# Reordering the opening of a fused attention and FFN kernel, and gating its last q tokens on the first weights

## The chip, the cores and the metric

One core of one Trainium2 chip. The metric is the device time of one execution in microseconds (us), lower is better. The fast executions of the kernel before lie between 326.11 and 326.97 us over all rounds; most kernels spread about as little, those with added dummy products up to 2 us. One run of the kernel before, of 372.13 us, with a low granted clock (0.851), is left out of every comparison.

## The reference

```python
pos = np.arange(S); theta = np.pi / 2.0 * pos / S
def phi(x): r = np.maximum(x, 0.0); return np.concatenate([r * cos_w, r * sin_w], axis=-1)
kv  = einsum('bhsf,bhsd->bhfd', phi(k), v);  z = sum of phi(k) over s
x   = (phi(q) @ kv) / (phi(q) @ z + 1e-6)      # [8 batches, 576 tokens, 8 heads x 64]
xn  = x / sqrt(mean(x*x) + 1e-6) * rms_g
g   = xn @ w_gate; out = (g * sigmoid(g) * (xn @ w_val)) @ w_out     # 512 -> 1536 -> 512
```

Everything is float32 outside and bf16 inside the products.

## The kernel before

The kernel loads k, q and v of batch 0, makes phi of them ("q_phi", "k_phi"), multiplies, divides, normalises token tiles of 128, transposes them on TensorE and feeds them to the FFN. Until the first token tile is normalised TensorE has little to do: this is the opening, about 30 us, with dummy products ("filler") that are meant to keep the clock up. After it TensorE is busy almost without a break. The parts that matter here:

```python
load_q_tokens(4, NJ)                 # tokens 4..8 of q, 640 KB, in the early queue
load_kv("k", 1, 0, 1)                # a quarter of k of batch 1
...
kvz_mm(0, low_banks, LOW)            # first half of phi(k)^T v
kvz_copy(A, 0, 0, low_banks[0], LOW); kvz_copy(A, 0, 1, low_banks[1], LOW)
v_cast(V, 0, 3, 4, 0, 5); v_cast(V, 0, 3, 4, 5, NJ)
...
filler(7, psV[1][:, :])
q_tr_pe(0, 2, psO[0][:, :])          # transposes of q tile 2
x_scale(0, 0)                        # normalise tile 0 (x * g was made ahead, x_gain)
...                                  # transposes of x tile 0, copies (x_tr)
q_phi(A, 0, 3, 1)                    # q tile 3, reads tokens 6 and 7
q_tr_evac(A, 0, 2, psO[0][:, :])
x_norm(0, 1)
q_phi(V, 0, 3, 0)
open_ffn(0, (0, 1), 0, 128)          # the first FFN products
x_tr_pe(0, 1, ...); x_tr_evac(V, 0, 1, ...)
q_tr_pe(0, 3, psO[1][:, :])
nd_pe(0, 2, psA); nd_post(0, 2, psA) # numerators of tile 2, division
q_tr_evac(A, 0, 3, psO[1][:, :])
open_ffn(0, (0, 1), 128, 256)
```

A is ScalarE, V is VectorE. In these traces the two work in the order in which their instructions are written: in the changed kernel ScalarE stands still for 5.0 us in front of one q_phi, with a copy that TensorE needs behind it.

Of the kernel before, what the change touches and what calls it, by code (L numbers as in the profile page):

```python
# [9 lines left out]
FP32 = mybir.dt.float32  # L10
# [16 lines left out]
def kernel(  # L27
# [11 lines left out]
    nc = tc.nc  # L39
# [34 lines left out]
    def load_kv(which, b, r0=0, r1=4, j0=0, j1=NJ):  # L74

        key = (which, b)
        if key not in raw:
            raw[key] = (two if which == "k" else one).tile(
                [P, 4, NJ * D], FP32, name=f"r{which}", tag=f"r{which}"
            )  # L80
        src = {"k": k, "v": v}[which]
        return nc.sync.dma_start(
            out=raw[key][:, r0:r1, j0 * D : j1 * D],
            in_=src[b, 2 * r0 : 2 * r1, :, :]
            .rearrange("h s d -> (h s d)")
            .rearrange("(r p n) -> p r n", p=P, n=NJ * D)[:, :, j0 * D : j1 * D],
        )
# [61 lines left out]
    def load_q_tokens(j0, j1):  # L149

        key = ("q", 0)
        if key not in raw:
            raw[key] = one.tile([P, 4, NJ * D], FP32, name="rq", tag="rq")
        return nc.sync.dma_start(
            out=raw[key][:, :, j0 * D : j1 * D],
            in_=q[0, :, :, :].rearrange("h s d -> (h s d)").rearrange(
                "(r p n) -> p r n", p=P, n=NJ * D
            )[:, :, j0 * D : j1 * D],
        )
# [7 lines left out]
    load_kv("v", 0, 2, 3)  # L167
    load_kv("v", 0, 3, 4, 0, 5)
    load_kv("v", 0, 3, 4, 5, NJ)
    load_q_tokens(4, NJ)  # L170
    load_kv("k", 1, 0, 1)
    nc.scalar.preload_act_table(AF.Silu)
    gb = one.tile([P, DM], FP32, name="gb")

# [106 lines left out]
            src = flat[:, 2048:2304].rearrange("p (i d) -> p i d", d=D)  # L281
        phi(eng, kp_of(b)[:, 8 * c : min(8 * c + 8, 36), o], src, f(c))

    def q_phi(eng, b, c, part):
        o = slice(0, D) if part == 0 else slice(D, F)
        f = cos_of if part == 0 else sin_of
        if (b, c) not in qp_tiles:
            qp_tiles[(b, c)] = four.tile(
                [P, H if c < 4 else 4, F], BF16, name="qp", tag="qp" if c < 4 else "qpt"
            )  # L290
        if b == 0:
            for i in range(2 if c < 4 else 1):
                j = 2 * c + i
                f = cos_of if part == 0 else sin_of
                phi(
                    eng, qp_tiles[(b, c)][:, 4 * i : 4 * i + 4, o],
                    raw[("q", 0)][:, :, j * D : (j + 1) * D], f(5 + j),
                )
            return
        src = view4(raw[("q", b)], c) if c < 4 else raw[("qt", b)][:, :, :]  # L300
        phi(eng, qp_tiles[(b, c)][:, :, o], src, f(c))
# [15 lines left out]
    def q_tr_pe(b, c, bank):  # L317
        t = qp_tiles[(b, c)]
        dst = bank.bitcast(BF16).rearrange("p (h s) -> p h s", s=P)
        for h in range(H if c < 4 else 4):  # L320
            nc.tensor.transpose(dst[:, h, :], t[:, h, :], ident[:, :])  # L321

    def q_tr_evac(eng, b, c, bank, heads=(0, 8)):
        h0, h1 = heads if c < 4 else (0, 4)
        if b == 0:
            src = bank.bitcast(BF16).rearrange("p (i h s) -> p h i s", i=2, h=H)
            copy(
                eng, q_dst(b, c)[:, h0:h1, :].rearrange("p h (i s) -> p h i s", i=2),
                src[:, h0:h1, :, :],
            )  # L330
            return
        dst = bank.bitcast(BF16).rearrange("p (h s) -> p h s", s=P)
        copy(eng, q_dst(b, c)[:, h0:h1, :], dst[:, h0:h1, :])
# [7 lines left out]
    def v_cast(eng, b, r0=0, r1=4, j0=0, j1=NJ):  # L341
        copy(
            eng, vvm[b % 2][:, r0:r1, j0:j1, 0:D],
            raw[("v", b)][:, r0:r1, j0 * D : j1 * D].rearrange("p r (j d) -> p r j d", d=D),
        )
# [50 lines left out]
    def kvz_copy(eng, b, c, bank, rs=(0, 4)):  # L396
        if (b, c) not in kvzs:
            kvzs[(b, c)] = three.tile([P, 4 * E], BF16, name="kvzs", tag=f"kvzs{c}")
        lo, hi = rs[0] * E, rs[1] * E
        copy(eng, kvzs[(b, c)][:, lo:hi], bank[:, lo:hi])  # L400
# [7 lines left out]
    def nd_pe(b, j, pst):  # L408

        o = headview(pst)  # L410
        for h in range(H):
            g, i = h // 4, h % 4
            if j < 4:
                nc.tensor.matmul(  # L414
                    o[:, g, i, :], lhsT=qpT[(b, 0)][:, h, j * P : (j + 1) * P],
                    rhs=kvz_of(b, h), start=True, stop=True,
                )
            else:
                for bb in (b - 1, b):
                    lo = 64 * (bb % 2)  # L420
                    r, c = (h // 2, h % 2) if bb == 0 else (i, g)
                    nc.tensor.matmul(  # L422
                        o[lo : lo + 64, g, i, :],
                        lhsT=qpT[(bb, 1)][:, r, 64 * c : 64 * c + 64],
                        rhs=kvz_of(bb, h), start=True, stop=True,
                    )
# [59 lines left out]
        rs_of[(b, j)] = rs  # L486

    xn_of = {}
    xg = three.tile([P, DM], FP32, name="sg", tag="sg")

    def x_gain(b, j, g):

        c = slice(g * DM // 2, (g + 1) * DM // 2)
        nc.vector.tensor_tensor(
            out=xg[:, c], in0=x_of[(b, j)][:, c], in1=gb[:, c], op=ALU.mult
        )

    def x_scale(b, j):
        xn = four.tile([P, DM], BF16, name="xn", tag="xn")
        nc.vector.tensor_scalar(  # L500
            out=xn[:, :], in0=xg[:, :], scalar1=rs_of[(b, j)][:, :], scalar2=None, op0=ALU.mult
        )
        xn_of[(b, j)] = xn

    def x_norm(b, j):
        xn = four.tile([P, DM], BF16, name="xn", tag="xn")
        nc.vector.scalar_tensor_tensor(  # L507
# [26 lines left out]
    def x_tr_evac(eng, b, j, bank, part=(0, 4)):  # L534
        dst = bank.bitcast(BF16).rearrange("p (t s) -> p t s", s=P)
        copy(eng, x_dst(b, j)[:, part[0] : part[1], :], dst[:, part[0] : part[1], :])
# [54 lines left out]
    def filler(n, bank):  # L591
        for _ in range(n):
            nc.tensor.matmul(bank, lhsT=warm[:, 0:P], rhs=warm[:, :], start=True, stop=True)  # L593
# [25 lines left out]
    def gval_slice(c0, c1):  # L619
        weight_dmas.append(weight_slice(wg, moe_w_gate, c0, c1))  # L620
        weight_dmas.append(weight_slice(wv, moe_w_val, c0, c1))
# [4 lines left out]
    )  # L626
    gval_slice(256, 512)
    gval_slice(512, 768)

    wo_dmas = []  # L630

# [19 lines left out]
    low_banks = [psG[1][:, :], psV[1][:, :]]  # L651
    high_banks = [psA[:, c, :] for c in range(2)]
    kvz_mm(0, low_banks, LOW)
    kvz_copy(A, 0, 0, low_banks[0], LOW)
    kvz_copy(A, 0, 1, low_banks[1], LOW)
    v_cast(V, 0, 3, 4, 0, 5)
    v_cast(V, 0, 3, 4, 5, NJ)
    kvz_mm(0, high_banks, (2, 3))
    nd_half(0, 0, 0, psV[0])
    nd_post_half(0, 0, 0, psV[0])  # L660
    x_gain(0, 0, 0)
    q_tr_evac(A, 0, 1, psO[0][:, :], (0, 4))
    kvz_mm(0, high_banks, (3, 4))
    kvz_copy(A, 0, 0, high_banks[0], HIGH)
    kvz_copy(A, 0, 1, high_banks[1], HIGH)
    filler(1, idle)
    nd_half(0, 0, 1, psO[1])
    nd_post_half(0, 0, 1, psO[1])
    q_tr_evac(A, 0, 1, psO[0][:, :], (4, 8))
    q_phi(A, 0, 2, 1)  # L670
    x_sq(0, 0)
    nd_pe(0, 1, psA)
    nd_post(0, 1, psA)
    x_gain(0, 0, 1)
    q_phi(A, 0, 2, 0)
    x_sq(0, 1)
    gval_slice(768, 1152)
    gval_slice(1152, 1536)
    filler(7, psV[1][:, :])
    q_tr_pe(0, 2, psO[0][:, :])  # L680
    x_scale(0, 0)

    def open_ffn(pair, steps, c0, c1, first=0, parts=(0, 1)):

        x = xnT[0]
        for i, n in enumerate(steps):
            for a in parts:
                w = (wg, wv)[a]
                bank = pairs[pair][a]
                lo = 256 * (first + i) + c0 % 256  # L690
                for t in range(NDT):
                    nc.tensor.matmul(  # L692
                        bank[:, lo : lo + c1 - c0],
                        lhsT=w[:, t, n * P : (n + 1) * P], rhs=x[:, t, c0:c1],
                        start=(t == 0), stop=(t == NDT - 1),
                    )
# [16 lines left out]
        x_tr_pe(0, 0, bank[:, :], part)  # L713
        x_tr_evac(eng, 0, 0, bank[:, :], part)
    q_phi(A, 0, 3, 1)
    q_tr_evac(A, 0, 2, psO[0][:, :])
    x_norm(0, 1)
    q_phi(V, 0, 3, 0)
    open_ffn(0, (0, 1), 0, 128)
    x_tr_pe(0, 1, psV[1][:, :])  # L720
    x_tr_evac(V, 0, 1, psV[1][:, :])
    q_tr_pe(0, 3, psO[1][:, :])
    nd_pe(0, 2, psA)
    nd_post(0, 2, psA)
    q_tr_evac(A, 0, 3, psO[1][:, :])
    x_sq(0, 2)
    wo_load(0)
    open_ffn(0, (0, 1), 128, 256)
    open_ffn(1, (2,), 0, 256, parts=(0,))
    nd_pe(0, 3, psA)  # L730
    nd_post(0, 3, psA)
    open_ffn(1, (3,), 0, 256, first=1, parts=(0,))
    x_norm(0, 2)
    open_ffn(1, (2, 3), 0, 256, parts=(1,))
    open_h(0, 0, 0)
# [34 lines left out]
    def at(blk, n, where, f, *args):  # L770
        slots.setdefault((blk, n), none())[where].append((f, args))
# [2 lines left out]
        for f, args in slots.get((blk, n), none())[where]:  # L774
            f(*args)

    d = load_kv("k", 1, 1, 4)
    tc.add_manual_dep(d.ins, weight_dmas[5].ins.name, SYNC_DEP, reason="after most weights")
    gate_q = load_q(1)
    tc.add_manual_dep(  # L780
# [10 lines left out]
    for j in range(NJ):  # L791
        at(0, 7 + max(0, j - 1) // 2, "post", k_phi, V, 1, j, 0)
        at(0, 7 + max(0, j - 1) // 2, "post", k_phi, A, 1, j, 1)
    at(0, 10, "post", q_phi, V, 1, 0, 0)
    at(0, 11, "post", q_phi, A, 1, 0, 1)


# [216 lines left out]
```

## Time and profile before

| | before |
|---|---|
| time, median | 326.53 us |
| span of the profiled run | 324.5 us |
| TensorE busy, granted clock | 97%, 0.999 |
| first FFN product | 17.26 us |
| start of the main loop | 29.98 us |
| from there to the end | 294.5 us |

TensorE bounds the kernel, so two numbers say most: when the main loop starts, and how long it is from there to the end. The lines that show it are in the prediction.

### The profile page before, as it was taken

The page shows a single profiled execution, that of the slowest core. Times are in us where ns is not written, and L with a number is a line of the kernel's source. Part 1 is how long each engine was busy: PE and PEld are TensorE (multiplying, and loading weights), DVE is VectorE, ACT ScalarE, POOL GpSimd, SP SyncE. Part 2 cuts the span into 40 slices and gives each one's busy share as a digit, 9 for nine tenths or more (in the row PEclk, how much of TensorE's full clock was granted, in tenths as well). Part 3 has the DMA queues.
Part 4 walks back from the last instruction along what each step waited for, and adds up shares of the span by engine and source line. Part 5 has one row for each costly group of instructions (what it writes and reads, how often), then busy time and mean ns, then how long its engine had stood idle before and what let it go on. Part 6 is the DMA issues. An engine that isn't in the chain of part 4 may idle for free.

```text
span 324.5 us, 6131 instructions
## 1 busy us (share of the span) xinstructions
PE 316.2 (97%) x2249; PEld 162.4 (50%) x2284; DVE 184.3 (57%) x398; ACT 173.8 (54%) x351; POOL 39.3 (12%) x85
## 2 busy tenths in 40 slices
PE   8999999999999999999999999999999999999995
PEld 3588465555445444554454445444544444444443
DVE  6875768787656765578267745772577133203410
ACT  6974865965665556645555466455644333223321
POOL 4660202001111110012001120120011000000000
PEclk9999999999999999999999999999999999999999
DMA  7999999898799775977597679856611400020014
GB/s 271 281 196 253 309 205 339 243 165 189 164 248 273 190 205 153 237 163 195 165 214 206 155 219 210 194 158 215 128 40 33 131 32 0 25 106 0 1 33 100
DMA packets 89377, 53.90 MB, mean 166 GB/s; under 512 B 56321, under 2 KB 81921, under 8 KB 89346
## 3 DMA queue, kind: packets, MB, share of 16 engines
q1 hardware_dynamic: 82304, 48.65, 57.4%
q0 software_dynamic: 6880, 4.72, 10.0%
q8 instruction: 18, 0.29, 0.4%
q10 hardware_dynamic: 162, 0.13, 0.2%
q14 instruction: 13, 0.11, 0.1%
HBM read 37.75 MB, written 9.44 MB: 145 GB/s over the span
## 4 chain that ended last, share of the span: by engine, by line
PE 93%; DVE 2%; ACT 2%; issue 1%; POOL 0%; DVEq 0%
PE psC L566 26%; PE psV L546 26%; PE psG L546 26%; PE psA L414 2%; PE psO L593 2%; PE psA L370 2%; PE psG L566 2%; PE psO L692 1%; PE psG L692 1%; PE psV L692 1%; PE psV L321 1%; ACT kpm L252 1%; PE psA L386 1%; ACT sg L555 0%; PE psA L422 0%
## 5 line engine op out<-in xcount | busy, mean ns | idle before, releaser
L561 DVE TENSOR_TENSOR hT<-psV,sg 128x512 bf16<-128x512 f32 x102 | 70.3, 689 | 96.0 <-PE psV L546 71.2
L555 ACT ACTIVATE sg<-psG 128x512 f32<-128x512 f32 x102 | 60.6, 594 | 64.5 <-PE psG L546 63.2
L546 PE MATMUL psV<-xnT,wv 128*128 128x512 bf16 (+1 forms) x365 | 92.1, 375 | 0.4
L546 PE MATMUL psG<-xnT,wg 128*128 128x512 bf16 (+1 forms) x352 | 90.9, 375 | 0.7
L566 PE MATMUL psC<-wo,hT 128*128 128x512 bf16 x382 | 88.2, 380 | 0.7
L546 PEld LDWEIGHTS <-wv 128*128 128x128 bf16 x416 | 40.6, 98 | 47.4
L566 PEld LDWEIGHTS <-hT 128*128 128x128 bf16 x420 | 40.2, 98 | 46.7
L546 PEld LDWEIGHTS <-wg 128*128 128x128 bf16 x416 | 38.5, 98 | 40.8 <-DVE xnT L339 0.4
L485 POOL TENSOR_TENSOR rs<-ms,mhalf 128x1 f32<-128x1 f32 x36 | 19.8, 549 | 187.6 <-ACT scr L480 187.6
L337 ACT COPY osb<-psC 128x512 f32<-128x512 f32 (+1 forms) x33 | 19.1, 579 | 43.1 <-PE psC L566 42.4
L507 DVE SCALAR_TENSOR_TENSOR xn<-xt,rs,gb 128x512 bf16<-128x512 f32 x35 | 26.5, 757 | 16.4 <-POOL rs L485 16.3
L480 ACT ACTIVATE scr<-xt 128x513 bf16<-128x513 f32 x36 | 22.9, 635 | 23.7 <-DVE xt L469 23.6
L252 ACT ACTIVATE kpm<-rk,tab 128x256 bf16<-128x256 f32 (+2 forms) x58 | 28.2, 545 | 1.5 <-DMA rk<-in_k_dram 1.5
L469 DVE TENSOR_TENSOR xt<-psA,rec 128x512 f32<-128x512 f32 x35 | 24.2, 691 | 1.2
L252 ACT ACTIVATE qp<-rq,tab 128x512 bf16<-128x512 f32 (+1 forms) x37 | 23.7, 661 | 0.0
L254 DVE TENSOR_SCALAR kpm<-rk,tab 128x128 bf16<-128x128 f32 (+2 forms) x64 | 20.5, 377 | 2.1 <-DMA rk<-in_k_dram 2.1
L254 DVE TENSOR_SCALAR qp<-rq,tab 128x512 bf16<-128x512 f32 (+1 forms) x37 | 16.0, 452 | 0.0
L414 PEld LDWEIGHTS <-qpT 128*128 128x128 bf16 x248 | 11.7, 98 | 6.7 <-issue 0.3
L414 PE MATMUL psA<-kvzs,qpT 128*128 128x65 bf16 x248 | 12.8, 194 | 0.3
L546 PE MATMUL psG<-xnt_tail,wg 128*128 128x512 bf16 x48 | 12.3, 379 | 0.1
L546 PE MATMUL psV<-xnt_tail,wv 128*128 128x512 bf16 x47 | 12.1, 379 | 0.0
L339 DVE CAST vvm<-rv 128x1024 bf16<-128x1024 f32 (+4 forms) x16 | 10.4, 674 | 0.0
(99 smaller groups left out, 183.8 us busy)
## 6 DMA issues: line engine op xcount, KB each, us to landing
out_dram<-osb SPq DMA_DIRECT2D x28, 256.0 KB, 2.5
rk<-in_k_dram SPq DMA_DIRECT2D x20, 256.0 KB, 3.2
rq<-in_q_dram SPq DMA_DIRECT2D x20, 256.0 KB, 3.1
rv<-in_v_dram SPq DMA_DIRECT2D x16, 256.0 KB, 3.2
rq<-in_q_dram SPq DMA_DIRECT2D x2, 1024.0 KB, 9.2
out_dram<-osb SPq DMA_DIRECT2D x14, 128.0 KB, 3.2
rv<-in_v_dram SPq DMA_DIRECT2D x3, 576.0 KB, 8.4
wo<-in_moe_w_out_dram POOLq DMA_DIRECT2D x4, 384.0 KB, 7.1
```

Of the source, the lines that this page charges most:

```text
L252: nc.scalar.activation(out=out_ap, in_=in_ap, func=AF.Relu, scale=scale)
L254: eng.tensor_scalar(out=out_ap, in0=in_ap, scalar1=scale, scalar2=0.0, op0=ALU.mult, op1=ALU.max)
L337: nc.scalar.copy(out=o, in_=i)
L414: nc.tensor.matmul(o[:, g, i, :], lhsT=qpT[(b, 0)][:, h, j * P : (j + 1) * P], rhs=kvz_of(b, h), start=True, stop=True,)
L469: nc.vector.tensor_tensor(out=xt[:, 0:DM].rearrange("p (b h d) -> p b h d", b=2, d=D), in0=o[:, :, :, 0:D], in1=rec[:, :, :].unsqueeze(3). ...
L480: nc.scalar.activation(out=scr[:, :], in_=xt[:, 0 : DM + 1], func=AF.Square, scale=1.0 / math.sqrt(DM), accum_out=ms[:, :],)
L485: nc.gpsimd.tensor_tensor(out=rs[:, :], in0=ms[:, :], in1=mhalf[:, :], op=ALU.pow)
L507: nc.vector.scalar_tensor_tensor(out=xn[:, :], in0=x_of[(b, j)][:, 0:DM], scalar=rs_of[(b, j)][:, :], in1=gb[:, :], op0=ALU.mult, op1=ALU. ...
L546: nc.tensor.matmul(pst[bank][:, cols[0] : cols[1]], lhsT=w[:, t, n * P : (n + 1) * P], rhs=x[:, t, cols[0] : cols[1]], start=(t == 0), sto ...
L555: nc.scalar.activation(out=sg[:, :], in_=psG[bank][:, :], func=AF.Silu)
L561: nc.vector.tensor_tensor(out=hTs[blk][:, n, :], in0=psV[bank][:, :], in1=sg[:, :], op=ALU.mult)
L566: nc.tensor.matmul(bank, lhsT=hTs[blk][:, n, j * P : (j + 1) * P], rhs=wo[:, n, :], start=(n == 0), stop=(n == NNT - 1),)
```

## The change

The intent, as the edit suggests it: get the early queue shorter so that weights come sooner (the last q tokens wait for the first weight slice: this wait is called the gate below), swap a v cast and two copies between ScalarE and VectorE, move half of q tile 2's phi from ScalarE to VectorE, and start the FFN products ahead of q tile 2's transposes. A step of the normalisation (x_gain, x_scale) is dropped for the plain x_norm, k of batch 1 comes in one piece, and one q_phi of batch 1 moves a step later.

```diff
-    load_q_tokens(4, NJ)
-    load_kv("k", 1, 0, 1)
+    load_q_tokens(4, 6)
...
     gval_slice(512, 768)
+    d = load_q_tokens(6, NJ)
+    tc.add_manual_dep(d.ins, weight_dmas[0].ins.name, SYNC_DEP, reason="after the first weights")
...
-    kvz_copy(A, 0, 0, low_banks[0], LOW)
-    kvz_copy(A, 0, 1, low_banks[1], LOW)
-    v_cast(V, 0, 3, 4, 0, 5)
+    kvz_copy(V, 0, 0, low_banks[0], LOW)
+    kvz_copy(V, 0, 1, low_banks[1], LOW)
+    v_cast(A, 0, 3, 4, 0, 5)
...
-    x_gain(0, 0, 1)
-    q_phi(A, 0, 2, 0)
+    q_phi(A, 0, 2, 1, (1,))
+    q_phi(V, 0, 2, 0, (0,))
+    x_norm(0, 0)
+    q_phi(V, 0, 2, 0, (1,))
...
-    filler(7, psV[1][:, :])
-    q_tr_pe(0, 2, psO[0][:, :])
-    x_scale(0, 0)
+    filler(9, psV[1][:, :])
...
     q_phi(A, 0, 3, 1)
-    q_tr_evac(A, 0, 2, psO[0][:, :])
     x_norm(0, 1)
-    q_phi(V, 0, 3, 0)
     open_ffn(0, (0, 1), 0, 128)
     x_tr_pe(0, 1, psV[1][:, :])
     x_tr_evac(V, 0, 1, psV[1][:, :])
+    q_tr_pe(0, 2, psO[0][:, :])
+    q_tr_evac(A, 0, 2, psO[0][:, :])
+    q_phi(V, 0, 3, 0)
+    open_ffn(0, (0, 1), 128, 256)
     q_tr_pe(0, 3, psO[1][:, :])
     nd_pe(0, 2, psA)
...
-    open_ffn(0, (0, 1), 128, 256)
...
-    d = load_kv("k", 1, 1, 4)
+    d = load_kv("k", 1)
...
-    at(0, 10, "post", q_phi, V, 1, 0, 0)
+    at(0, 11, "post", q_phi, V, 1, 0, 0)
```

Left out of the diff: the removal of x_gain and x_scale themselves, the first x_gain, one filler, the first `q_phi(A, 0, 2, 1)` cut to its first half, the new argument of q_phi that names the half, and an FFN step moved from behind nd_pe(0, 3) to before it.

More of the change, by code (lines that the diff above doesn't have):

```diff
@@ L282, in k_phi_as_q, with q_phi @@
         phi(eng, kp_of(b)[:, 8 * c : min(8 * c + 8, 36), o], src, f(c))
-    def q_phi(eng, b, c, part):
+    def q_phi(eng, b, c, part, subs=(0, 1)):
         o = slice(0, D) if part == 0 else slice(D, F)
@@ L291, in q_phi @@
         if b == 0:
-            for i in range(2 if c < 4 else 1):
+            for i in subs if c < 4 else (0,):
                 j = 2 * c + i
@@ L488 @@
     xn_of = {}
-    xg = three.tile([P, DM], FP32, name="sg", tag="sg")
-    def x_gain(b, j, g):
-        c = slice(g * DM // 2, (g + 1) * DM // 2)
-        nc.vector.tensor_tensor(
-            out=xg[:, c], in0=x_of[(b, j)][:, c], in1=gb[:, c], op=ALU.mult
-        )
-    def x_scale(b, j):
-        xn = four.tile([P, DM], BF16, name="xn", tag="xn")
-        nc.vector.tensor_scalar(
-            out=xn[:, :], in0=xg[:, :], scalar1=rs_of[(b, j)][:, :], scalar2=None, op0=ALU.mult
-        )
-        xn_of[(b, j)] = xn
     def x_norm(b, j):
@@ L628 @@
     gval_slice(512, 768)
+    d = load_q_tokens(6, NJ)
+    tc.add_manual_dep(
+        d.ins, weight_dmas[0].ins.name, SYNC_DEP, reason="after the first weights"
+    )
     wo_dmas = []
@@ L660 @@
     nd_post_half(0, 0, 0, psV[0])
-    x_gain(0, 0, 0)
     q_tr_evac(A, 0, 1, psO[0][:, :], (0, 4))
@@ L665 @@
     kvz_copy(A, 0, 1, high_banks[1], HIGH)
-    filler(1, idle)
     nd_half(0, 0, 1, psO[1])
@@ L669 @@
     q_tr_evac(A, 0, 1, psO[0][:, :], (4, 8))
-    q_phi(A, 0, 2, 1)
+    q_phi(A, 0, 2, 1, (0,))
     x_sq(0, 0)
@@ L727 @@
     wo_load(0)
-    open_ffn(0, (0, 1), 128, 256)
     open_ffn(1, (2,), 0, 256, parts=(0,))
+    open_ffn(1, (3,), 0, 256, first=1, parts=(0,))
     nd_pe(0, 3, psA)
     nd_post(0, 3, psA)
-    open_ffn(1, (3,), 0, 256, first=1, parts=(0,))
     x_norm(0, 2)
```

## The prediction

> **What bounds the kernel now.** I read the page first (busy shares, slices, chain), then the chain in order of time, then the timeline of the first 30 us, then what the DMA queues moved in short windows. From the page:
>
> ```profile
> span 324.5 us, 6131 instructions
> ...
> PE 316.2 (97%) x2249; PEld 162.4 (50%) x2284; DVE 184.3 (57%) x398; ACT 173.8 (54%) x351; POOL 39.3 (12%) x85
> ...
> PEclk9999999999999999999999999999999999999999
> ...
> PE 93%; DVE 2%; ACT 2%; issue 1%; POOL 0%; DVEq 0%
> ```
>
> TensorE is busy 97% of the span at a full granted clock and holds 93% of the chain that ended last. The change touches only the first 30 us and some loads; from there the stream of products is the same. So the time moves only by how much earlier or later TensorE gets through the opening, one to one. The opening's own chain shows where it waits for others:
>
> ```profile
> 14.56 0.72 ACT scr L480 x2
> ...
> 16.77 0.56 POOL rs L485
> 17.33 0.02 issue
> 17.36 0.75 DVE xn L507
> 18.11 0.82 DVE qp L254 x2
> 18.93 0.14 issue
> 19.07 0.38 PE psO L321 x4
> 19.45 0.25 PE psA L414 x8
> ```
>
> From 19.07 us on the opening's chain is TensorE alone; the stretch from 19.3 to 30.0 us has 10.70 us of TensorE busy in 10.70. Before that, TensorE is kept occupied by dummy products (fillers) and waits for token tile 0 to be normalised:
>
> ```profile
> 15.37 0.57 POOL L485 TENSOR_TENSOR rs<-ms,mhalf 128x1 f32<-128x1 f32 x1 [0.65 <-ACT scr L480]
> ...
> 15.97 0.49 DVE L500 TENSOR_SCALAR xn<-sg,rs 128x512 bf16<-128x512 f32 x1
> ...
> 16.51 0.28 PE L532 MATMUL psG<-ident,xn 128*128 128x128 bf16 x2
> ...
> 17.10 0.91 ACT L252 ACTIVATE qp<-rq,tab 128x256 bf16<-128x256 f32 x2
> 17.26 0.38 PE L692 MATMUL psG<-xnT,wg 128*128 128x128 bf16 x4 [0.35 <-ACT xnT L337]
> ```
>
> The first FFN product starts at 17.26 and waits for xnT on ScalarE, not for weights: the first gate slice, issued at 10.07, landed 4.9 us later, at 14.97; the first value slice (11.00 + 6.0) at 17.0. No TensorE wait on a DMA is in the waits of the first 40 us. The line at 17.10 is where tokens 6 and 7 of q are first read.
>
> **What the Trainium skill says.** (1) "DMA: Bandwidth & Descriptors", section "Queues, rings and completion order": each DMA engine takes turns between the queue rows that have work, a packet at a time. In the trace, the hardware queue (k of batch 1, 864 KB) and the software queue (weights) in 26.25 to 29.5 us:
>
> ```profile
> q1 hardware_dynamic: 325, 0.75, 66.0%
> q0 software_dynamic: 331, 0.25, 48.1%
> ```
>
> One packet each in turn, so that agrees. But that load was issued at 22.46 and the hardware queue moved nothing from 22.5 to 26 us, while weights ran: 3.5 us to its first packet. (2) The same page, "Anatomy of one DMA — SWDGE (gpsimd) path", puts about 2 us of fixed cost on one transfer. For the gated q load of batch 1 (issued at 30.84) the first packet came about 2 us later, so the trace gives 2 to 3.5 us, before any data. (3) "VectorE: DVE Perf Modes", "Why `tensor_tensor` can't do 2×_2P or 4×": two tensor inputs leave no read port for a double rate. The trace agrees: 757 ns for the 128x512 normalisation with two tensors, 486 ns for the scaling with one. (4) "TensorE: Matmul & The Clock Gate", "What's actually happening": the clock drops to half after about 3.4 us without work. The first 15 fillers took 6.01 us (0.4 each), later ones 0.21 each, which fits; no drop later is in the trace before.
>
> **The change part by part.**
>
> *LOW copies to VectorE, first piece of the last v cast to ScalarE.* A 128x260 copy from PSUM on VectorE took 427 ns and a 128x512 one 692, a slope of 1.05 ns per element, so 128x130 is estimated at 0.29 us, as against 0.27 on ScalarE. VectorE starts the next instruction some 0.08 us before the last ends, so: last LOW product 11.58, copies to 12.10, then the remaining cast (284 ns) to 12.30. Before, both casts were done at 11.99, and the HIGH products began at 12.26, behind the half of numerators that waits for the copies. Now they begin at about 12.34. Cost 0.08.
>
> *x_gain removed, x_scale becomes x_norm.* Two VectorE products of 0.42 go. The first sat in 13.30 to 13.72, just ahead of the reciprocal of the second half (13.64). With it gone the second half can start as soon as its numerators end: 13.50 + 0.08 = 13.58, so the 0.08 is won back, and x_sq stays at about 14.55, rs at 15.94. The second lay under the wait for rs and was free. Its replacement there, one q_phi of 0.35 on VectorE (15.42 to 15.77), is free too. But after rs the normalisation takes 0.757 in place of 0.486: 15.97 to 16.72. Cost 0.25: transposes at 16.76, first FFN product at 17.26 + 0.25 = 17.51.
>
> *q tile 2's transposes moved behind the first FFN products.* Eight transposes are 0.45 us of TensorE (chain: psO L321 x8, 0.45). They ran at 15.74, in time otherwise empty; the fillers grow from 8 to 9 to cover it. Now they lie in the busy stretch: 0.45 us more of work there. The useful work from the first FFN product to the first step of the main loop sums to 12.20 before (24 groups, 0.22 for four 128-column products, 0.44 for four of 256, 0.45 for eight transposes, 0.25 for eight numerators) out of 12.72 elapsed (17.26 to 29.98), so 0.52 was waiting. It becomes 12.65.
>
> *Numerators of tile 2 come later.* They stood after x_tr(1) and q tile 3 and ended at 19.70; now q tile 2 and FFN columns 128 to 256 (0.89) come first. With nothing waiting for q: FFN 17.51 to 18.40, x_tr(1) to 18.62, q tile 2 to 19.07, wait for xnT to 19.30, FFN to 20.19, q tile 3 to 20.64, numerators end at about 21.05. From there to the transposes of x tile 2 there is a chain of 3.53 us (before: 19.70 to 23.23): divide, square, power, nd_post of tile 3, normalise. TensorE has 2.91 us of work to cover it (0.88 + 0.29 + 0.87 + 0.87), as against 3.8 before. So x tile 2 is transposed at 24.58 and not 23.3: 1.25 us late, even with q in time.
>
> *The last q tokens gated on the first gate slice.* Out of the early queue go 384 KB of q and 288 KB of k. The weights hardly gain: their first packet came at 12.0, and the hardware queue was nearly empty by 12.4, so about 0.4 us: slice at 14.5. The q load is then issued at 14.5; first packet 2 to 3.5 us later, 16.5 to 18; 512 packets of 768 B over 16 engines, 32 each, alternating with weight packets. A weight packet took 16/370 us = 43 ns, a 768 B packet at the early rate of 390 GB/s 32 ns; 32 pairs are 2.4 us. End at 18.9 to 20.4, landing some 0.5 to 1 later: 19.4 to 21.4, middle 20.2. It is read at 17.10 (ScalarE) and 18.03 (VectorE) now. ScalarE is in order, so the copy of q tile 2 stands behind it: landing 20.2, two q_phi of 0.9 to 21.1, copy of 1.0 to 22.1, numerators of tile 2 to 22.5 in place of 21.05. That adds 1.45.
>
> *k of batch 1 in one piece, q_phi of batch 1 a step later.* 288 KB more behind the weights, landing about 33 in place of 31.0; it is first read at 33.26, and everything before that shifts later as well. Off the path.
>
> **Sum:** 1.25 + 1.45 = 2.7 us late by the working, of 326.6: 329.3. The gate could be less late than I put it, so I take 328.5.
>
> **Rivals.** *A: q lands in time.* The early queue is lighter, the first slice could land before 14, and a first packet after 2 us and a short drain give 18.9. For: the author moved q tile 3 behind more FFN work, as if they knew. Against: 3.5 us to a first packet in the trace. Then the loss is 1.25, or 0.5 if the chain to x tile 2 is shorter than before: 327.1 to 327.9. *B: the change gains.* The chain ahead of the first FFN product could shrink by more than the 0.25 that x_norm costs, as ScalarE is freed of the LOW copies and of half of q_phi. For: the chain of waits runs through just that q_phi at 15.28. Against: the sums of ScalarE at 14.56 wait for xt on VectorE, not for ScalarE; and the saved wait is at most the 0.52 us in the busy stretch. Time 326.0 to 326.5. *C: the clock.* A wait of 2 us with breaks around it could bring TensorE to half rate for some 3.4 us, a cost of 1.7 more: 330.5 to 331.
>
> **Range and chances.** Between B's end and C's start: 326.4 to 330.6. A 2% gain needs 6.5 us, more than half of the opening's busy stretch and 0.52 us of it is wait: 0.01. A 2% loss needs C and a late q together: 0.03. Within 2%: 0.96. I put 0.75 on slower at all.
>
> **What would show it.** In the changed profile: first FFN product near 17.5; normalisation of tile 0 at 0.75; the q load of 384 KB issued near 14.5 and landing near 20; a wait of ScalarE and VectorE on the DMA of rq ahead of q_phi; a hole in TensorE of 1 to 2 us between 20 and 23, and a second of 0.6 before the transposes of x tile 2; the main loop starting near 32.3 and not 29.98; the same length after it. I am wrong if no wait on rq is there, or if the first FFN product is earlier than 17.2, or if the distance from the main loop's start to the end differs by over 0.5 us.

## The result

| | before | changed |
|---|---|---|
| time, median of 6 | 326.53 us | 332.59 us |
| span of the profiled run | 324.5 us | 330.9 us |
| granted clock | 0.999 | 0.994 |
| first FFN product | 17.26 | 17.81 |
| start of the main loop | 29.98 | 35.74 |
| from there to the end | 294.5 | 295.2 |

The ratio is 1.0186, 95% interval 1.0173 to 1.0199. Ratios here are the mean time of one kernel's fast runs over that of the other's of the same rounds, so not quite the ratio of the medians. The change makes the kernel 6.06 us slower, and the measured time lies above the range of the prediction. Of the 6.4 us between the spans, 5.76 are there when the main loop starts; 0.64 come later. The weights hardly gained: the first slice landed at 14.65 and not 14.97, and no compute engine had waited for it.

The page of the changed kernel:

```profile
span 330.9 us, 6164 instructions
...
PEclk9998999999999999999999999999999999999999
...
PE 88%; DMA 6%; DVE 2%; ACT 2%; issue 1%; SPq 0%; DVEq 0%
```

A DMA share of 6% has come into the chain that ended last, and one slice of the clock is below 9 tenths. The opening's part of that chain, in order of time (start, length, what):

```profile
2.27 7.63 DMA rv<-in_v_dram
9.91 0.30 issue
10.21 4.45 DMA wg<-in_moe_w_gate_dram
14.65 0.02 issue
14.67 8.07 DMA rq<-in_q_dram
22.75 0.02 issue
22.77 0.91 ACT qp L251 x2
23.67 0.91 ACT qpT L336
24.58 0.05 issue
24.62 0.62 PE psA L413 x8
```

Three loads stand in a row: the first v, the weight slice gated on it, the q load gated on the slice. That last one took 8.07 us from issue to landing. Before, the first v and the slice were no part of the chain, which had TensorE's dummy products and the VectorE and ScalarE steps there. The waits of the first 48 us that bear on it (engine, who, for whom: total, times, longest), first of the kernel before:

```profile
PEld L321 <- ACT qp L252: 0.9, 2, 0.7
...
PE psO L321 <- DVE qp L254: 0.2, 1, 0.2
```

and of the changed kernel:

```profile
ACT qp L251 <- DMA rq<-in_q_dram: 5.0, 1, 5.0
...
DVE qp L253 <- DMA rq<-in_q_dram: 3.2, 1, 3.2
...
PE psO L320 <- ACT qp L251: 2.7, 1, 2.7
...
PE psV L320 <- DVE qp L253: 0.5, 1, 0.5
```

ScalarE and VectorE wait for q, TensorE waits behind ScalarE for 2.7 us. The last line is another wait, in the main loop at 47 us. TensorE in single microseconds of the changed kernel (stretch, length, busy, instructions, granted clock, DMA share, GB/s):

```profile
20.00:21.00 1.00, 0.66 (x12) 1.00 1.25 238
21.00:22.00 1.00, 0.00 (x0) 1.00 1.31 239
22.00:23.00 1.00, 0.00 (x0) 1.00 1.43 197
23.00:24.00 1.00, 0.67 (x7) 0.64 1.34 202
24.00:25.00 1.00, 0.74 (x11) 0.50 1.32 204
25.00:26.00 1.00, 1.00 (x10) 0.50 1.31 202
26.00:27.00 1.00, 1.00 (x14) 0.66 1.32 204
27.00:28.00 1.00, 1.00 (x15) 1.00 1.30 230
```

A hole of 2.7 us (20.66 to 23.33), and some 3.4 us at half clock (23.27 to 26.69, by finer windows). Before, these microseconds are full at clock 1.00; two of them:

```profile
22.00:23.00 1.00, 1.00 (x11) 1.00 1.32 204
24.00:25.00 1.00, 1.00 (x17) 1.00 1.35 215
```

What the two DMA queues moved between the issue of the q load and its landing (packets, MB, share), q1 being the hardware queue with q and q0 the weights; first 14.5 to 18.5 us, then 18.5 to 22.5:

```profile
q0 software_dynamic: 1196, 0.60, 127.3%
```

```profile
q0 software_dynamic: 1011, 0.50, 92.0%
q1 hardware_dynamic: 528, 0.39, 39.4%
```

q moved nothing in the first of these. By finer windows its first packet came at 18.73, 4.1 us after the issue at 14.67; until then some 1230 weight packets went through 16 DMA engines, 77 each. Then its 528 packets shared the engines with the weights for 3.8 us, and 0.2 later it had landed.

### The profile page after: what moved, and what is told of

Its sections match the earlier page's. It is cut to its first block, busy times and chain, and to the rows that moved or that the text cites. A ratio compares the mean times of both kernels' runs of the same rounds, so it can differ in the third digit from the quotient of the medians.

```text
span 330.9 us, 6164 instructions
## 1 busy us (share of the span) xinstructions
PE 320.3 (97%) x2285; PEld 163.5 (49%) x2285; DVE 184.9 (56%) x399; ACT 173.1 (52%) x348; POOL 39.3 (12%) x85
## 4 chain that ended last, share of the span: by engine, by line
PE 88%; DMA 6%; DVE 2%; ACT 2%; issue 1%; SPq 0%; DVEq 0%
PE psC L549 26%; PE psG L529 26%; PE psV L529 25%; DMA rq<-in_q_dram 2%; PE psA L413 2%; DMA rv<-in_v_dram 2%; PE psA L369 2%; DMA wg<-in_moe_w_gate_dram 1%; PE psG L549 1%; PE psG L677 1%; PE psO L677 1%; ACT kpm L251 1%; PE psV L320 1%; PE psA L385 1%; DVE hT L544 1%
## 5 line engine op out<-in xcount | busy, mean ns | idle before, releaser
L529 PE MATMUL psG<-xnT,wg 128*128 128x512 bf16 (+1 forms) x368 | 92.8, 374 | 0.1
L549 PE MATMUL psC<-wo,hT 128*128 128x512 bf16 x396 | 89.4, 379 | 0.0
L490 DVE SCALAR_TENSOR_TENSOR xn<-xt,rs,gb 128x512 bf16<-128x512 f32 x36 | 27.3, 757 | 16.5 <-POOL rs L484 16.5
L251 ACT ACTIVATE qp<-rq,tab 128x512 bf16<-128x512 f32 (+1 forms) x35 | 22.9, 670 | 5.0 <-DMA rq<-in_q_dram 5.0
L253 DVE TENSOR_SCALAR kpm<-rk,tab 128x128 bf16<-128x128 f32 (+2 forms) x64 | 20.5, 378 | 2.3 <-DMA rk<-in_k_dram 2.3
L253 DVE TENSOR_SCALAR qp<-rq,tab 128x512 bf16<-128x512 f32 (+1 forms) x39 | 16.4, 441 | 3.2 <-DMA rq<-in_q_dram 3.2
L338 DVE CAST vvm<-rv 128x1024 bf16<-128x1024 f32 (+3 forms) x15 | 10.3, 709 | 0.0
```

The lines of the kernel that those rows point to most:

```text
L251: nc.scalar.activation(out=out_ap, in_=in_ap, func=AF.Relu, scale=scale)
L253: eng.tensor_scalar(out=out_ap, in0=in_ap, scalar1=scale, scalar2=0.0, op0=ALU.mult, op1=ALU.max)
L490: nc.vector.scalar_tensor_tensor(out=xn[:, :], in0=x_of[(b, j)][:, 0:DM], scalar=rs_of[(b, j)][:, :], in1=gb[:, :], op0=ALU.mult, op1=ALU. ...
L529: nc.tensor.matmul(pst[bank][:, cols[0] : cols[1]], lhsT=w[:, t, n * P : (n + 1) * P], rhs=x[:, t, cols[0] : cols[1]], start=(t == 0), sto ...
L549: nc.tensor.matmul(bank, lhsT=hTs[blk][:, n, j * P : (j + 1) * P], rhs=wo[:, n, :], start=(n == 0), stop=(n == NNT - 1),)
```

## The experiments

Theory: the gate makes most of the loss, because a load on the hardware queue that is issued behind a backlog of weight packets waits for them; the reordering and the moved q_phi make the rest. Rivals: the reordering makes most of it; or the half clock does; or a load simply takes this long.

**1. Gate undone.** From the changed kernel:

```diff
     load_q_tokens(4, 6)
+    load_q_tokens(6, NJ)
...
-    d = load_q_tokens(6, NJ)
-    tc.add_manual_dep(d.ins, weight_dmas[0].ins.name, ...)
```

> The changed kernel with the gate alone undone: the q load of 384 KB stands in the early queue right after its sister of 256 KB. Theory (the gate makes the loss): no wait on the DMA of rq, no hole in TensorE after 20 us, clock 1.00 throughout; what is left is the reordering, the later first product (17.8) and the longer normalisation: 326.5 + 1.25 + 0.3 = 328.1 us, between 327.5 and 328.5. Rival (the reordering and the other parts hold most of the 6 us): 331 or more.

Measured: 328.26 us (ratio 1.0055, 1.0039 to 1.0071), main loop at 31.24, clock 1.00, no engine waits for rq ahead of q_phi. So the gate is worth 332.59 - 328.26 = 4.3 of the 6.1 us (4.3 by the ratios too). The main loop starts 1.26 later than before, where the prediction's working without a late q had 1.25. The remaining 0.6 us lie after that.

**2. Gate alone, on the kernel before.**

```diff
-    load_q_tokens(4, NJ)
+    load_q_tokens(4, 6)
...
+    d = load_q_tokens(6, NJ)
+    tc.add_manual_dep(d.ins, weight_dmas[0].ins.name, ...)
```

> The kernel before with the gate alone added (q tokens 4 and 5 early, 6 to 8 after the first gate slice). Theory: q lands near 22.7; in the order of before the transposes of q tile 3 come 1.3 us of TensorE work earlier, so the hole is longer (18.6 to 23.3), the numerators of tile 2 end near 25.0 in place of 19.7, and the clock falls: 326.5 + 5.3 + about 2 = 333.8 us, between 332.5 and 335. Rival (gate harmless without the reordering): 326.5 to 328.

Measured: 333.34 us (ratio 1.0208, 1.0192 to 1.0224), main loop at 37.22. The gate alone costs 6.8 us, more than the whole change: the order of before has less TensorE work to do until q arrives. The reordering of the change thus hides part of what its gate costs. TensorE here:

```profile
20.00:21.00 1.00, 0.00 (x0) 1.00 1.24 242
21.00:22.00 1.00, 0.00 (x0) 0.89 1.33 227
22.00:23.00 1.00, 0.00 (x0) 0.50 1.42 200
...
27.00:28.00 1.00, 1.00 (x10) 0.50 1.26 251
```

It is idle from 18.96, and the clock falls at 21.77, 2.8 us later; in the changed kernel it fell 2.6 us into the hole. The Trainium skill ("TensorE: Matmul & The Clock Gate", "What's actually happening") names an idle window of about 3.4; both falls came sooner than that.

**3. Gate moved to the first v load.**

```diff
-    tc.add_manual_dep(d.ins, weight_dmas[0].ins.name, ...)
+    tc.add_manual_dep(d.ins, first_v.ins.name, ...)
```

> The changed kernel with the q load gated on the first v load (landed 10.2) and not on the first gate slice (14.65). Theory A (a load on the hardware queue waits behind the weight packets already queued on each DMA engine): issued at 10.2, ahead of all weight packets, its first packet comes about 2 us later, it lands before 16, no engine waits for it and the time is that of the ungated kernel within 0.3 us. Theory B (8 us from issue to landing whatever else is queued): lands at 18.3, q_phi of tile 3 waits 0.5 us, time 0.3 to 0.8 us over the ungated one.

Measured: 328.52 us (ratio 1.0066, 1.0048 to 1.0084). The load was issued at 9.67 and landed 3.4 us later:

```profile
rq<-in_q_dram SPq DMA_DIRECT2D x1, 384.0 KB, 3.4
```

Issued ahead of every weight packet (their first came after 12.25), though with its own queue's earlier loads still running, the same 384 KB took 3.4 and not 8.07 us, which rules out that the load takes 8 us in any case. No engine waits for it.

**4. Gate kept, backlog taken away.**

```diff
     gval_slice(0, 256)                       # gated on v, as before
+    d = load_q_tokens(6, NJ)                 # gated on the first slice, as in the change
     gval_slice(256, 512)
+    tc.add_manual_dep(weight_dmas[2].ins, d.ins.name, ...)
     gval_slice(512, 768)
```

> The changed kernel, gate kept, but the weight slices after the first pair wait until the gated q load has landed, so that only one slice is queued when q is issued at about 14.6. The time is not the question (the later slices come late, 330 to 334 us). Theory A (q waits behind the weight packets that are already queued when it is issued): first q packet about 2 us after issue, landing at 18.5 or earlier, 4 us from issue. Theory B (4 us to the first packet in any case): first packet at 18.5, landing after 20, 6 us or more from issue.

Measured: issued at 13.80, landed 3.8 us later (time 335.77 us, one run of unknown state: GpSimd stood 6.65 us until q had landed, to issue the next slice, and only then made the `rs` that the first normalisation needs, so the first FFN product came at 23.15; the time says nothing here, the queues do). The queues from the issue to 14.75 us, and from there to 17.5:

```profile
q0 software_dynamic: 289, 0.14, 110.3%
```

```profile
q1 hardware_dynamic: 528, 0.39, 54.2%
q0 software_dynamic: 1, 0.00, 0.1%
```

The q packets begin 1.0 us after the issue, when the 289 packets left of the one queued slice (18 an engine) are through. So how long q waits depends on what is queued ahead of it. But it does not wait for all of it. What was queued can be estimated from the sizes (512 packets for a slice of 256 KB, 768 for one of 384 KB, from 0.60 MB in 1196 packets) less the packets already moved; the 36 are counted, and the 165 leave out a slice of w_out that was just being issued:

| load, kernel | weight packets an engine queued at the issue (estimate) | moved before its first packet | wait for its first packet |
|---|---|---|---|
| gated q, this experiment | 18 | 18 | 1.0 us |
| q of batch 1, kernel before (30.84) | 36 | 29 | 2.1 us |
| gated q, changed kernel | 144 | 77 | 4.1 us |
| k of batch 1, kernel before (22.46) | 165 | 60 | 3.6 us |

Where the limit lies and what sets it stays open.

**5. q_phi of batch 1 back at its step**, on the ungated kernel:

```diff
-    at(0, 11, "post", q_phi, V, 1, 0, 0)
+    at(0, 10, "post", q_phi, V, 1, 0, 0)
```

> The ungated kernel with VectorE's first q_phi of batch 1 put back at step 10 (the change had moved it to step 11). Theory: in the changed kernel the transposes of q tile 0 of batch 1 wait 0.48 us for that q_phi, and from the main loop's start to the end it is 295.16 us against 294.52 before; with the move undone the wait goes and the time falls by 0.6 us from the ungated 328.26, to 327.65. Rival (the 0.6 us comes from the later k and v loads): no change, 328.2.

Measured: 327.57 us (ratio 1.0037, 1.0024 to 1.0051), 0.7 below the ungated kernel, or 0.6 by the ratios, as the two ran in different rounds. From the main loop to the end it is 294.5 again, and the wait `PE psV L320 <- DVE qp L253`, which the ungated kernel still had, is gone; a move of one instruction by one step is worth a tenth of the whole loss.

**6. TensorE's order of before as well**, on the last kernel: q tile 2's transposes ahead of the first FFN products, numerators of tile 2 ahead of FFN columns 128 to 256. Left out of this diff: the same for one FFN step and nd_pe(0, 3), and VectorE's order, which went back with it (q_phi of tile 2 whole ahead of the first x_norm, q_phi of tile 3 right after the second).

```diff
-    filler(9, psV[1][:, :])
+    filler(7, psV[1][:, :])
+    q_tr_pe(0, 2, psO[0][:, :])
...
+    q_tr_evac(A, 0, 2, psO[0][:, :])         # after q_phi(A, 0, 3, 1), as before
...
-    q_tr_pe(0, 2, psO[0][:, :])
-    q_tr_evac(A, 0, 2, psO[0][:, :])
-    open_ffn(0, (0, 1), 128, 256)
     q_tr_pe(0, 3, psO[1][:, :])
     nd_pe(0, 2, psA)
...
+    open_ffn(0, (0, 1), 128, 256)
```

> As the last one, and TensorE's order of before as well: q tile 2's transposes ahead of the first FFN products, numerators of tile 2 ahead of FFN columns 128 to 256. Theory (the reordering costs its 0.45 us of transposes in the busy stretch and 0.6 us ahead of x tile 2): main loop starts at 30.2 and not 31.24, time 326.7 us, within 0.3 of the kernel before; what is left of the loss is the 0.2 us of the longer normalisation. Rival (the first part, casts and copies, holds a further loss): 327.3 or more.

Measured: 326.42 us (ratio 1.0005, 0.9992 to 1.0017). The reordering, TensorE's and VectorE's together, is worth 327.57 - 326.42 = 1.15 us. What is left of the change (casts, copies, the longer normalisation, k in one piece) cannot be told from nothing; the 0.2 us expected of the normalisation are within the noise.

**7. Dummy products in the hole**, 13 and then 9, in the changed kernel:

```diff
+    filler(13, psO[1][:, :])                 # or 9
     q_tr_pe(0, 3, psO[1][:, :])
```

> The changed kernel with 13 dummy products of 128x512 in the hole ahead of q tile 3's transposes (13 x 0.216 = 2.8 us, no longer than the hole itself). Theory: some 1.7 us of the 6.06 is the half clock from 23.4 to 26.7; the dummies keep the clock at 1.00, q lands as late as ever (22.7): 332.6 - 1.7 = 330.9 us. Rival (clock is no cost, or follows the transposes): 332.6 unchanged.

Measured: 332.69 us (331.32 to 333.32; ratio 1.0184, 1.0153 to 1.0215). The clock stayed at 1.00, the median did not fall. The profiled run is the fastest of the four, 331.32: its gate opened earlier (q issued at 13.91) and q landed at 21.85, not as late as ever. From the numerators of tile 2 (23.73) to the main loop (34.38) it took 10.65 us, against 24.62 to 35.74, 11.12, in the changed kernel. So the half clock costs this stretch 0.5 us and not 1.7; the other 0.9 of the earlier main loop is the earlier q.

> The changed kernel with 9 dummy products in the hole (1.9 us, over before q lands, so that they can hold nothing up; 13 of them had given 331.3 to 333.3). Theory: the half clock costs the changed kernel only 0.5 us, as the stretch from the numerators of tile 2 to the main loop took 11.12 us in it and 10.65 with 13 dummies; with 9 the clock stays at 1.00 and the time is 332.59 - 0.5 = 332.1 us. Rival (1.7 us, as predicted): 330.9. Rival (dummies do not help at all): 332.6.

Measured: 332.68 us (331.86 to 333.77; ratio 1.0193, 1.0173 to 1.0213); no gain in time. The main loop started at 35.19, 0.55 us earlier than in the changed kernel, at the same landing of q within 0.1, and the clock held:

```profile
24.00:25.00 1.00, 0.50 (x11) 1.00 1.31 200
```

Yet the span is the same within 0.1: 0.47 of the 0.55 were lost at 104 us (experiment 8 shows how).

**8. Dummies with the gate alone.** 18 of them, in the kernel of experiment 2.

> The kernel before with the gate alone and 18 dummy products (3.9 us) in its hole of 4.3 us. Theory: there the half clock costs more, since TensorE alone bounds the stretch after the hole: 12.45 us from the numerators of tile 2 to the main loop against 10.69 before. With the clock held at 1.00: 333.34 - 1.76 = 331.6 us. Rival (no help): 333.3.

Measured: 332.25 us (331.57 to 333.43; ratio 1.0181, 1.0160 to 1.0203), the median 1.1 below experiment 2, though the intervals overlap a little. The main loop started at 35.38 and not 37.22, 1.84 us earlier where 1.76 were expected. At 104 us TensorE then waits for GpSimd's copy of the last v of batch 3, and GpSimd for its DMA:

```profile
103.34 1.19 POOL L339 CAST vvt<-rv 64x256 bf16<-64x256 f32 x2 [7.54 <-DMA rv<-in_v_dram]
...
104.12 0.19 PE L370 MATMUL psA<-vvt,kpm 128*128 128x65 bf16 x1 [0.96 <-POOL vvt L339]
```

The same place in the profile of 9 dummies has a wait of 0.32 us. In the kernels with the late q and no dummies TensorE arrives later and does not wait. So a faster stretch ran into a load whose issue had hardly moved with it: the v loads were issued 0.30 us earlier than in experiment 2 and GpSimd's copy began at 103.34 and not 103.81, for a TensorE that was 1.84 earlier. The profiled run of 13 dummies has no wait there (copy begun at 102.00), and its whole lead reached the end: main loop 1.36 us and span 1.4 us ahead of the changed kernel. That the spread of the timed runs comes from this wait was not shown; only one run of each kernel is profiled.

**9. A version that may beat both.** The kernel before has a wait of its own: the transposes of q tile 3 wait for VectorE's q_phi. One edit puts half of that q_phi into VectorE's idle time (16.46 to 16.95):

```diff
     x_scale(0, 0)
+    q_phi(V, 0, 3, 0, (0,))
...
-    q_phi(V, 0, 3, 0)
+    q_phi(V, 0, 3, 0, (1,))
```

> The kernel before with one edit: VectorE's q_phi of tile 3 split in its two halves, the first put into VectorE's idle 0.49 us ahead of the copy of xnT (16.46 to 16.95), so that the transposes of q tile 3 need not wait for it (0.3 us of TensorE idle around 18.9). Expected: main loop starts 0.2 to 0.35 us earlier (29.65 to 29.8), time 326.2 us. Rival (the copy of q tile 2 on ScalarE ends at 18.91 and takes the wait's place): gain under 0.1 us.

Measured: 325.98 us against 326.36 (ratio 0.9990, 0.9978 to 1.0003). Run again unaltered:

> The version that beat the kernel before by 0.1%, unaltered, for a second interval: 326.0 us against 326.4, ratio 0.9988. If the first gain was chance: ratio 1.000.

Measured: 326.08 us against 326.39 (ratio 0.9992, 0.9979 to 1.0004). Both medians are 0.3 to 0.4 us lower, and both intervals still reach 1.000, so the gain of 0.1% is likely but not clear of noise. The main loop was expected at 29.65 to 29.8; it started at 29.98 and 29.75. Counted from the first FFN product, which came later in both, it took 12.41 and 12.40 us against 12.72 before: this stretch did get 0.3 us shorter. The wait for VectorE is gone from TensorE's waits between 15 and 45 us. In the kernel before:

```profile
PE psG L692 <- ACT xnT L337: 0.3, 1, 0.3
PE psO L321 <- ACT qp L252: 0.2, 1, 0.2
PE psO L321 <- DVE qp L254: 0.2, 1, 0.2
```

and in this one:

```profile
PE psG L693 <- ACT xnT L337: 0.3, 1, 0.3
PE psO L321 <- ACT qp L252: 0.2, 1, 0.2
```

## Why the prediction was wrong

The direction and the place were right; the size was not. By its own steps:

- *The late q*: "End at 18.9 to 20.4, landing some 0.5 to 1 later: 19.4 to 21.4, middle 20.2." This is the step that failed. The mechanism was right, a load behind the weights that ScalarE and VectorE wait for; its two terms were too small. The gate came nearly as predicted (14.67, predicted 14.5). The first packet came after 4.1 us (predicted 2 to 3.5), and draining and landing took 4.0 (predicted 2.4 and 0.5 to 1). q landed at 22.75, 2.55 after the middle. The two loads of the trace before from which 2 and 3.5 us came were no range of one cost: the load of 2 us met a short backlog, that of 3.5 us one like the new load's (the table in experiment 4), so 3.5 was the case to go by and not the upper end. The skill's 2 us of fixed cost, set beside them, was no support: the page has it for the software queue and puts most of it after the last byte, not before the first. The drain's 32 pairs assumed that all DMA engines start together; the q packets set in over a microsecond and tail off over another.
- *The final discount*: "The gate could be less late than I put it, so I take 328.5." No number stood behind it. The working's own sum was 329.3.
- *q_phi of batch 1 a step later*: "Off the path." Wrong: 0.6 to 0.7 us, shown by experiment 5. The prediction's own sign, a length after the main loop's start that differs by over 0.5 us, came: 0.64. It had looked at when k lands and not at who waits for this q_phi.
- *The reordering*: 1.25 with q in time, of which 0.25 for the normalisation. Right: the ungated kernel's main loop starts 1.26 later, and experiment 6 has 1.15 for the order. That the first agrees within 0.01 is luck, as single profiles are sure to some 0.2; counted from the first FFN product the stretch grew from 12.72 to 13.77, 1.05 for the order.
- *The normalisation, the casts and the copies*: 0.25 and nothing on balance; the first FFN product of the ungated kernel came at 17.47, 0.21 late. The normalisation did take 0.75 us and not 0.49, but what it cost is not shown: 0.21 is no more than the spread between profiles, and experiment 6, which keeps it, is level with the kernel before.
- *Rival C, the clock*: it came, though the range ended where it would begin; but its 1.7 us was 0.5 at the main loop's start in the changed kernel, where the steps of ScalarE and VectorE to x tile 2 hold much of the chain through that stretch. In experiment 2, where TensorE is busy through most of it at half clock, it was 1.84. That the chain explains the difference is argued, not tested. In neither did the whole of it show in the time.

With the measured terms put in, the working gives 2.7 + 2.55 (late q) + 0.64 (after the main loop's start) + 0.5 (clock) = 6.4 us, and the spans differ by 6.4. Each term has a run behind it, but with 0.2 us of doubt in a profile such a close fit is partly luck.

The landing of q alone carries the time out of the range: 329.3 + 2.55 = 331.85, against an upper end of 330.6. The clock followed from it and was taken as a rival, not as a consequence: without the late q the hole and the half clock are gone (experiment 1). The prediction also set its first 15 fillers (0.4 us each) down to a low clock; the profile's clock column reads 1.00 there, so only their length speaks for it.

## What to carry to other kernels

Before gating a load behind other loads, count what will be queued ahead of it at that moment: a load that took 3.4 us ahead of all weights took 8.1 us behind five queued weight slices, and nothing in the kernel before was waiting for the weights that the gate meant to favour. Estimate the wait of a load from one with the same backlog, and do not average it with one that met less. And when TensorE will stand still for some microseconds (2.6 were enough here), add the clock to it, then ask whether TensorE or another engine bounds the stretch in which it is low, and which load the regained time will meet next.

## What the Trainium skill lacked or had wrong

- "DMA: Bandwidth & Descriptors", "Queues, rings and completion order": once a load has begun in full, the turns between the queues are as the page says (44 to 49 packets of each in every quarter of a microsecond, in the changed kernel from 20 to 21 us). But from the page's round robin one would expect a new load to begin almost at once. Here it began only after 77 packets an engine of the other queue (4.1 us), 60 for the k load of the kernel before (3.6 us), 18 where no more was queued (1.0 us). The page says that an engine drains one packet of a ring before it switches, 9 to 17 descriptors as a rule and 64 at most. If the trace counts descriptors, 60 is within that ceiling and 77 is over it; no run here shows whether this is the cause.
- The same page, "Anatomy of one DMA — SWDGE (gpsimd) path": its 2 us of fixed cost, meant for the software queue, is no use as an estimate for a load of the hardware queue that meets a backlog: 8.07 us for 384 KB behind five slices, 3.4 us ahead of them. No page says what a load waits behind a backlog.
- "TensorE: Matmul & The Clock Gate", "What's actually happening": the page names an idle window of about 3.4 us before the clock falls. Here it fell 2.6 and 2.8 us after the last product (changed kernel, gate alone). It then stayed low for 3.4 and 6.8 us, about one and two such windows. No page says what this costs where other engines hold part of the chain: 0.5 us at the main loop's start in the changed kernel, 1.84 with the gate alone.
